# Scores of the last head pair on half the array each: a bucketed attention followed by a channel mix, one core

## The chip, the cores and the metric

The kernel runs on one core of a Trainium2 chip. The metric is the device time of one launch in microseconds (us). The kernel before takes 245.62 us, the median of two runs (245.34 and 245.9). A core has five engines with a queue each: PE (matmul, with its own weight loads), DVE (vector), ACT (activation), POOL (a second, slower vector engine) and SP, which here issues DMAs. Matmuls write to PSUM, 128 partitions of eight banks with 512 float32 columns each; everything else lies in SBUF.

## The reference

Inputs are q, k and v (4 batches, 8 heads, 768 positions, 64 values each), a projection of 64 x 6, and the weights of a channel mix. Each query and key gets a 6-bit bucket from the signs of its projection. Attention is restricted to pairs of equal buckets:

```python
q_bucket = np.sum(q_bits * powers, axis=-1)          # q_bits = (q @ proj) > 0
mask = q_bucket[:, :, :, None] == k_bucket[:, :, None, :]
scores = scale * np.matmul(q, k.transpose(0, 1, 3, 2))
scores = np.where(mask, scores, -1000000000.0)
attn = softmax(scores)                               # written out in the reference
out = np.matmul(attn, v)
```

The heads' outputs are put side by side (x, 4 x 768 x 512), and a channel mix follows:

```python
xk = mu_k * x + (1.0 - mu_k) * x_prev                # x_prev: x one position earlier
xr = mu_r * x + (1.0 - mu_r) * x_prev
k = np.maximum(xk @ w_k, 0.0)
return sigmoid(xr @ w_r) * (k * k @ w_v)
```

## The kernel before, in words

The 32 heads are worked on as 16 pairs (0 to 15), four pairs to a batch. For each pair the kernel does the following.

- **Load and split** (L323, L391, L394). q and k of both heads come in as float32 with 128 partitions. DVE writes a float16 rounding ("hi", 64 columns) and the remainder ("lo", 64 columns) side by side into `nh`. For pairs 4 to 15 one instruction each covers q and k of both heads, 1536 columns.
- **Transpose** (L398). One DMA transposes `nh` to `a`: for each of four blocks (q of head 0, q of head 1, k of head 0, k of head 1) 128 rows by 768 positions, hi in rows 0 to 63 and lo in rows 64 to 127.
- **Bucket bits** (L418, L421, L438). PE multiplies the four blocks with the projection, each on 32 columns of the array, DVE turns the result's signs into values of fixed size, and POOL copies six rows per block over rows 64 to 69 of `a`, over part of lo. One matmul over 128 rows then gives the score plus a bucket term that is large where all six signs agree.
- **Scores** (`add_scores`, L522 to L546). The transposed scores of a pair, 2 heads x 6 key chunks of 128 x 768 queries, are 9216 columns. They are made in nine steps of 1024 columns, named sc15_0 to sc15_8 for pair 15, each into a slot of two PSUM banks. Columns run through head 0 first, then head 1, so a step is cut at every 512 and 768 columns: two or three matmuls (L536). One ACT instruction per step takes the exponential and writes it to `pt` (L540).
- **PV** (`add_pv`, L548 to L613). For each head three groups of twelve matmuls, two key chunks in each (L563): weights are 128 x 128 blocks of `pt`, and 65 columns (v and a column of ones) stream. Head 0 needs steps 0 to 4, head 1 steps 4 to 8. DVE divides by the sum (L576, L577, L581). The result is transposed by a DMA (L597) or, for pair 15 and the first four, on PE (L591).
- **Mix** (`add_mix`, `add_moe`). DVE makes xk and xr (L622 to L636). After a batch's four pairs the channel mix runs: L651 (keys), L671 (gates) and L684 (values) on PE, ACT's relu and tanh (L655, L674), DVE's square and product (L658, L691), and the output DMAs (L694).

The order of the work is written out by hand: every operation gets a number as it is added to a plan, and the list `ORDER` (L17) names all of them in the order in which they are issued, engine by engine first in, first out. `BANKS` (L72) names the PSUM place of each result. The durations that `add` gets play no part in the order. Around pair 15 the order interleaves its nine score steps, one at a time, with those of pairs 13 and 14, PV groups, and the channel mix of batches 1 and 2. Pair 15's steps stand in the order 2, 6, 1, 5, 3, 4, 0, 7, 8. Behind step 7 follow PV's first group of head 1, three groups of head 0, step 8, eight L684, PV's second group of head 1, four L671, and PV's last group.

Of the kernel before, what the change touches and what calls it, by code (L numbers as in the profile page):

```python
# [8 lines left out]
FP32 = mybir.dt.float32  # L9
# [3 lines left out]
AF = mybir.ActivationFunctionType  # L13
ALU = mybir.AluOpType
# [66 lines left out]
]  # L81

# [46 lines left out]
def kernel(  # L129
# [35 lines left out]
    FIRSTS = (0, 1)  # L165
    ROW_SP = ()
    OT_PE = (0, 1, 2, 3, 15)
    QS = 4.0
    ESC = (D ** -0.5) / (QS * QS)
    BITW = 4096.0  # L170
# [13 lines left out]
    nh_t = [buf([P, 4 * NSC, P], FP16, f"nh{i}") for i in range(NNH)]  # L184
    a_t = [buf([P, 4, S], FP16, f"a{i}") for i in range(NAQ)]
    side_nat = {s: [t[:, 2 * i : 2 * i + 2, :] for t in nat_t] for i, s in enumerate("qk")}
    side_nh = {s: [t[:, 2 * NSC * i : 2 * NSC * (i + 1), :] for t in nh_t] for i, s in enumerate("qk")}
    side_a = {s: [t[:, 2 * i : 2 * i + 2, :] for t in a_t] for i, s in enumerate("qk")}
    bx_t = [buf([P, S], FP16, f"bx{i}") for i in range(NBX)]
# [117 lines left out]
    def add_load(n):  # L307
        b, t = divmod(n, NPB)
        s = n % NQ
        for side in "qk":  # L310
            if n == 0:
                for j in range(2):
                    lq = "ACT" if side == "k" and j == 0 else "SP"

                    def f(side=side, j=j, lq=lq):
                        (nc.scalar if lq == "ACT" else nc.sync).dma_start(out=side_nat[side][s][:, j, :],
                                      in_=SRC[side][b, 2 * t + j].rearrange("(p c) d -> p (c d)", c=NSC))
                        if lq == "ACT":
                            nc.scalar.dma_start(out=pj, in_=proj)
                    add(lq, 0.42, f, at=0.75, w=[("nat", side, s, j)] + (["pj"] if lq == "ACT" else []), svc=0.5, name=f"ldq{n}{side}{j}")  # L320
            else:
                def f(side=side):
                    nc.sync.dma_start(out=side_nat[side][s],  # L323
                                      in_=SRC[side][b, 2 * t : 2 * t + 2].rearrange("j (p c) d -> p j (c d)", c=NSC))
                add("SP", 0.5, f, at=0.75, w=[("nat", side, s, j) for j in range(2)], svc=1.05, name=f"ldq{n}{side}")

        def fv():
            nc.sync.dma_start(out=vn_t[n % NV],
                              in_=v[b, 2 * t : 2 * t + 2].rearrange("j (p c) d -> p j (c d)", c=NSC))
        add("SP", 0.5, fv, at=0.75, w=[("vn", n % NV)], svc=1.05, name=f"ldv{n}")  # L330
# [52 lines left out]
    def add_prep(n):  # L383
        s, sh, sa = n % NQ, n % NNH, n % NAQ
        whole = n in MERGED
        for side in ("qk",) if whole else "qk":
            nat, nh, a = (nat_t[s], nh_t[sh], a_t[sa]) if whole else (side_nat[side][s], side_nh[side][sh], side_a[side][sa])
            m = len(side)

            def hi(nat=nat, nh=nh):  # L390
                nc.vector.tensor_scalar(out=nh[:, :, 0:D], in0=nat.rearrange("p j (c d) -> p (j c) d", d=D), scalar1=QS, scalar2=None, op0=ALU.mult)  # L391

            def lo(nat=nat, nh=nh):
                nc.vector.scalar_tensor_tensor(out=nh[:, :, D:P], in0=nat.rearrange("p j (c d) -> p (j c) d", d=D),  # L394
                                               scalar=QS, in1=nh[:, :, 0:D], op0=ALU.mult, op1=ALU.subtract)

            def tr(nh=nh, a=a):
                nc.sync.dma_start_transpose(out=a.rearrange("p j (c q) -> p (j c) q", q=P), in_=nh.rearrange("p c d -> p (c d)"))  # L398
            rn = [("nat", x, s, j) for x in side for j in range(2)]
            nh_h = [("nhh", x, sh, j) for x in side for j in range(2)]  # L400
            nh_l = [("nhl", x, sh, j) for x in side for j in range(2)]
            ax = [("a", x, sa, j) for x in side for j in range(2)] + [("ab", x, sa, j, h) for x in side for j in range(2) for h in range(2)]
            add("DVE", DVE_C(768 * m, 2), hi, r=rn, w=nh_h, port=1, name=f"hi{n}")
            add("DVE", DVE_C(768 * m), lo, r=rn + nh_h, w=nh_l + [("nz", sh)], port=1, name=f"lo{n}")
            add("SP", 1.86 if whole else 1.46, tr, r=nh_h + nh_l, w=ax, svc=2.95 if whole else 1.57, tr=1, name=f"tr{n}")
        add_bits(n, [("q", 0), ("q", 1), ("k", 0), ("k", 1)])

    def add_bits(n, blocks):
# [4 lines left out]
        def f(nm=nm):  # L413
            ps = ps_t[plan.slot[nm]]
            for w_, st in ((p1, True), (p2, False)):
                for lo, hi in ((0, 512), (512, S)):
                    for i, (side, j) in enumerate(blocks):
                        nc.tensor.matmul(ps[32 * i : 32 * i + 32, lo:hi], w_, side_a[side][sa][:, j, lo:hi], start=st, stop=not st)  # L418

        def g(nm=nm):  # L420
            nc.vector.tensor_scalar(  # L421
# [7 lines left out]
        for i, (side, j) in enumerate(blocks):  # L429
            w = [("ab", side, sa, j, h) for h in range(2)]  # L430
            if n in ROW_SP:
                def row(i=i, side=side, j=j):
                    nc.sync.dma_start(out=side_a[side][sa][D : D + NB, j, :], in_=bx_t[sx][32 * i : 32 * i + NB, :])
                add("SP", 0.72, row, r=[("bx", sx)], w=w, svc=0.17, name=f"row{n}{side}{j}")
                continue

            def row(i=i, side=side, j=j):
                nc.gpsimd.tensor_copy(side_a[side][sa][D : D + NB, j, :].bitcast(FP32), bx_t[sx][32 * i : 32 * i + NB, :].bitcast(FP32))  # L438
            add("POOL", 0.55, row, r=[("bx", sx)], w=w, port=1, name=f"row{n}{side}{j}")

    def add_prep_turn(n):
# [74 lines left out]
    def pieces(s):  # L516
# [2 lines left out]
                      | {x for x in range(0, 2 * NSC * S + 1, S) if lo < x < hi})  # L519
        return list(zip(cuts[:-1], cuts[1:]))  # L520

    def add_scores(n):  # L522
        sa, sp = n % NAQ, n % NPT
        for s in range(NSTEP):
            nm = f"sc{n}_{s}"
# [22 lines left out]
    def add_pv(n):  # L548
# [3 lines left out]
        for j in range(2):  # L552
            nm = f"oo{n}_{j}"
            for g in range(3):
                def f(nm=nm, j=j, g=g):
                    oo = sm(nm)
                    if uc and g == 0:
                        nc.tensor.matmul(oo[:, 0:390].rearrange("p (c e) -> p c e", e=65), tiny,
                                         vsu_t[n % NVS][:, j, :].unsqueeze(1).to_broadcast([P, NSC, D + 1]), start=True, stop=False)
                    for jc in (2 * g, 2 * g + 1):  # L560
                        for ic in range(NSC):
                            o = j * NSC * S + jc * S + ic * P
                            nc.tensor.matmul(oo[:, ic * 65 : ic * 65 + 65], pt_t[sp][:, o : o + P], va_t[sa][:, j, jc, 0 : D + 1],  # L563
                                             start=(not uc and ic == 0 and jc == 0), stop=(ic == NSC - 1 and jc == NSC - 1))
                lo = j * NSC * S + 2 * g * S
                steps = range(lo // STEP, (lo + 2 * S - 1) // STEP + 1)
                add("PE", 12 * 0.0315, f, r=[("pt", sp, s) for s in steps] + [("va", sa, j), ("va1", sa)] + (["tiny", ("vs", n % NVS)] if uc else []),
                    w=[(nm,)], take=("sm", nm, 0) if g == 0 else None, name=nm)
            sr = (2 * n + j) % NRC
# [195 lines left out]
```

## Time and profile before

| | |
|---|---|
| median of two runs | 245.62 us (245.34 to 245.9) |
| span of the profiled execution, first to last instruction | 243.0 us |
| time outside the span, median less span | 2.6 us |
| PE busy | 234.2 us, 96% |
| DVE busy | 187.6 us, 77% |
| ACT busy | 182.6 us, 75% |
| POOL busy | 95.9 us, 39% |
| L536, matmuls of the scores, 384 in all, 24 of them pair 15's | 79.2 us with overlaps |
| granted PE clock over the span | 1.000 |

The profile is of one execution, and no time of it other than its span is given. Times in its rows are counted from the first instruction. Lines L... are those of the kernel before. Matmuls are pipelined: the next starts before the last has run out, so durations of PE's rows overlap, and what a matmul costs is read from one start to the next. A value in brackets at a row's end is the idle time of the engine before it and what ended it.

### The profile page before, as it was taken

Reading aid. Unit: us, or ns where it says so; the run is one execution under the profiler, and the core shown is the slowest. Engines: PE = TensorE matmul, PEld = TensorE weight load, DVE = VectorE, ACT = ScalarE, POOL = GpSimd, SP = SyncE. Lnnn points to the kernel's source line nnn. Section 1 sums busy time; section 2 is a strip of 40 time slices with the busy share of each in tenths; the row PEclk is TensorE's granted clock in tenths of the full one; section 3 lists DMA queues with packets and bytes.
Section 4 is the critical chain, followed back from the end, with each engine's and each line's share of the span. In section 5 each row is a group of like instructions: output and inputs, shape, how many; then the busy total and the mean of one; then the engine's idle time right before and its main releaser. Section 6 shows DMA issues by size and latency. Waiting matters only on the chain.

```text
span 243.0 us, 6250 instructions
## 1 busy us (share of the span) xinstructions
PE 234.2 (96%) x2522; PEld 147.3 (61%) x2522; DVE 187.6 (77%) x388; ACT 182.6 (75%) x242; POOL 95.9 (39%) x150
## 2 busy tenths in 40 slices
PE   8998999999999899999999999999999999999994
PEld 6975676765567446465556665465566765455443
DVE  3489899999899989699999989936745476966142
ACT  3689999999989689698877998777679871165230
POOL 5465797885919673428036230093500000000000
PEclk9999999999999999999999999999999999999999
DMA  6989999999999999999989683464310403041033
GB/s 229 370 243 197 219 259 230 356 204 348 245 217 233 367 281 208 259 272 264 222 195 233 155 162 85 146 114 126 120 46 0 35 3 119 0 173 47 0 131 132
DMA packets 72526, 44.01 MB, mean 181 GB/s; under 512 B 54832, under 2 KB 67504, under 8 KB 72496
## 3 DMA queue, kind: packets, MB, share of 16 engines
q1 hardware_dynamic: 72272, 43.40, 70.7%
q8 instruction: 20, 0.33, 0.6%
q10 hardware_dynamic: 224, 0.20, 0.2%
q14 instruction: 10, 0.08, 0.1%
HBM read 24.12 MB, written 6.29 MB: 125 GB/s over the span
## 4 chain that ended last, share of the span: by engine, by line
PE 55%; DVE 6%; DMA 3%; issue 1%; DVEq 0%
PE ps_all L684 15%; PE ps_all L651 13%; PE ps_all L536 11%; PE ps_all L671 8%; PE ps_all L563 6%; DMA a<-nh 3%; PE ps_all L418 2%; DVE xk L636 1%; DVE tm L633 1%; DVE nh L391 1%; DVE nh L394 1%; DVE df L622 0%; DVE os L691 0%; DVE va L373 0%; DVE bx L421 0%
## 5 line engine op out<-in xcount | busy, mean ns | idle before, releaser
L540 ACT ACTIVATE pt<-ps_all 128x1024 bf16<-128x1024 f32 x144 | 139.1, 1040 | 19.8 <-PE ps_all L536 18.7
L536 PE MATMUL ps_all<-a 128*128 128x256 f16 (+1 forms) x384 | 79.2, 325 | 2.0 <-ACT pt L540 1.1
L438 POOL COPY a<-bx 6x384 f32<-6x384 f32 x56 | 38.9, 696 | 54.5 <-DVE bx L421 42.3
L563 PEld LDWEIGHTS <-pt 128*128 128x128 bf16 x1152 | 43.7, 97 | 11.6 <-issue 2.1
L651 PE MATMUL ps_all<-xk,wk 128*128 128x384 bf16 x256 | 49.6, 326 | 0.3 <-DVE xk L636 0.3
L536 PEld LDWEIGHTS <-a 128*128 128x128 f16 x384 | 33.7, 98 | 24.9 <-issue 3.5
L684 PE MATMUL ps_all<-wv,k 128*128 128x512 bf16 (+2 forms) x208 | 46.7, 363 | 0.0
L563 PE MATMUL ps_all<-va,pt 128*128 128x65 bf16 x1152 | 46.2, 193 | 0.4 <-DVE va L373 0.4
L658 DVE TENSOR_TENSOR k<-kr 128x384 bf16<-128x384 bf16 x64 | 25.8, 424 | 14.1 <-ACT kr L655 13.8
L655 ACT ACTIVATE kr<-ps_all 128x384 bf16<-128x384 f32 x64 | 29.6, 497 | 7.7 <-PE ps_all L651 6.7
L651 PEld LDWEIGHTS <-wk 128*128 128x128 bf16 x256 | 24.0, 98 | 15.5 <-issue 0.3
L674 ACT ACTIVATE rs<-ps_all 128x512 f32<-128x512 f32 x24 | 14.3, 603 | 23.0 <-DVE os L691 11.7
L684 PEld LDWEIGHTS <-k 128*128 128x128 bf16 x208 | 19.6, 98 | 19.1
L691 DVE SCALAR_TENSOR_TENSOR os<-rs,ps_all 128x512 f32<-128x512 f32 (+2 forms) x26 | 16.7, 643 | 14.9 <-PE ps_all L684 10.8
L394 DVE SCALAR_TENSOR_TENSOR nh<-nat,nh 128x1536 f16<-128x1536 f32 (+1 forms) x16 | 25.7, 1607 | 0.2
L671 PE MATMUL ps_all<-wr,xr 128*128 128x512 bf16 x96 | 24.5, 379 | 0.0
L349 POOL TENSOR_TENSOR vt<-vn 128x384 f32<-128x384 f32 x12 | 14.4, 1200 | 10.8 <-DMA vn<-in_v_dram 7.1
L581 DVE TENSOR_TENSOR ob<-ps_all,rc 128x384 bf16<-128x384 f32 x32 | 17.5, 552 | 0.7
L391 DVE TENSOR_SCALAR nh<-nat 128x1536 f16<-128x1536 f32 (+1 forms) x16 | 15.8, 989 | 1.5 <-DMA nat<-in_k_dram 0.9
L671 PEld LDWEIGHTS <-xr 128*128 128x128 bf16 x96 | 8.7, 97 | 9.5 <-issue 0.6
L421 DVE TENSOR_SCALAR bx<-ps_all 128x768 uint16<-128x768 uint16 x14 | 13.3, 952 | 1.2 <-PE ps_all L418 0.8
L373 DVE SCALAR_TENSOR_TENSOR va<-ps_all,vn 128x384 bf16<-128x384 f32 x24 | 12.8, 549 | 1.4 <-ACT pt L540 0.9
(77 smaller groups left out, 190.6 us busy)
## 6 DMA issues: line engine op xcount, KB each, us to landing
vn<-in_v_dram SPq DMA_DIRECT2D x16, 384.0 KB, 5.1
out_dram<-os SPq DMA_DIRECT2D x23, 256.0 KB, 2.5
nat<-in_q_dram SPq DMA_DIRECT2D x15, 384.0 KB, 4.6
nat<-in_k_dram SPq DMA_DIRECT2D x15, 384.0 KB, 5.3
wst<-in_moe_w_k_dram SPq DMA_DIRECT2D x2, 512.0 KB, 7.2
wst<-in_moe_w_r_dram SPq DMA_DIRECT2D x2, 512.0 KB, 6.2
wst<-in_moe_w_v_dram SPq DMA_DIRECT2D x2, 512.0 KB, 5.9
k<-in_moe_w_k_dram SPq DMA_DIRECT2D x1, 512.0 KB, 7.8
```

Source lines behind the costliest of these rows:

```text
L391: nc.vector.tensor_scalar(out=nh[:, :, 0:D], in0=nat.rearrange("p j (c d) -> p (j c) d", d=D), scalar1=QS, scalar2=None, op0=ALU.mult)
L394: nc.vector.scalar_tensor_tensor(out=nh[:, :, D:P], in0=nat.rearrange("p j (c d) -> p (j c) d", d=D), scalar=QS, in1=nh[:, :, 0:D], op0=AL ...
L438: nc.gpsimd.tensor_copy(side_a[side][sa][D : D + NB, j, :].bitcast(FP32), bx_t[sx][32 * i : 32 * i + NB, :].bitcast(FP32))
L536: nc.tensor.matmul(ps[:, lo - s * STEP : hi - s * STEP], side_a["k"][sa][:, j, jc * P : (jc + 1) * P], side_a["q"][sa][:, j, q0 : q0 + hi ...
L540: nc.scalar.activation(out=pt_t[sp][:, s * STEP : (s + 1) * STEP], in_=ps_t[plan.slot[nm]], func=AF.Exp, bias=EBIAS, scale=ESC)
L563: nc.tensor.matmul(oo[:, ic * 65 : ic * 65 + 65], pt_t[sp][:, o : o + P], va_t[sa][:, j, jc, 0 : D + 1], start=(not uc and ic == 0 and jc ...
L581: nc.vector.tensor_tensor(out=ob_t[so][:, :, j * D : (j + 1) * D], in0=oo[:, :, 0:D], in1=rc_t[sr][:, 1, :].unsqueeze(2).to_broadcast([P, ...
L651: nc.tensor.matmul(ps[:, 0:HALF], wk_sb[:, d, fc * P : (fc + 1) * P], xk_t[mx[d]][:, h * HALF : (h + 1) * HALF], start=(d == 0), stop=(d = ...
L655: nc.scalar.activation(out=kr_t[sk], in_=sm(nm)[:, 0:HALF], func=AF.Relu, scale=0.5 ** 0.5)
L658: nc.vector.tensor_tensor(out=k2_t[s2][:, h * HALF : (h + 1) * HALF], in0=kr_t[sk], in1=kr_t[sk], op=ALU.mult)
L671: nc.tensor.matmul(sm(nr), xr_t[mx[d]][:, c * P : (c + 1) * P], wr_sb[:, d, :], start=(d == 0), stop=(d == NDC - 1))
L684: nc.tensor.matmul(sm(nv)[:, x0:x1], k2_t[(b * NFC + fc) % NK2][:, c * P : (c + 1) * P], wv_sb[:, fc, x0:x1], start=(fc == 0), stop=(fc == ...
```

## The change

For pair 15 alone (`TILED = (15,)`), the two heads are laid on different halves of the array's rows.

- The four blocks are stored in the order q of head 0, k of head 0, q of head 1, k of head 1 (`til_nat`, `til_a`), and head 1 has its hi in rows 64 to 127 and its lo in rows 0 to 63. DVE's hi and lo are two instructions of 768 columns each instead of one of 1536. The six bucket rows of head 1 go to rows 0 to 5 and those of head 0 to rows 64 to 69.
- A score step holds 512 columns of head 0 in one bank of the slot and 512 of head 1 in the other. Steps 0, 1 of every three are one key chunk by the first 512 queries, step 2 the last 256 queries of both chunks. A step is a matmul of 64 rows per head and key chunk, and then one of six rows per head and key chunk that adds the bucket term: 4 or 8 matmuls instead of 2 or 3, each with its weight load, 48 instead of 24 for the pair.
- The lo part is not used in the scores of this pair. Before, lo rows 70 to 127 stood in the sum with lo of the other side.
- PV reads `pt` by the new places. Each group g of either head needs steps 3g, 3g+1 and 3g+2.
- `ORDER` keeps the places of the steps and their exps, which now run from 0 to 8 in turn. In PE's queue, head 0's third PV group stands behind step 8, where it stood ahead of it.

```diff
-    ... 1220, 1216, 1221, 1217, 1218, 998, ...
+    ... 1220, 1216, 1217, 1218, 1221, 998, ...
```

In these numbers 1220 and 1221 are head 0's second and third PV group, 1216 is the exp of step 7, 1217 and 1218 are step 8 and its exp, and 998 is the first four of the eight L684.

```diff
+    til_nat = {s: [t.rearrange("p (j i) x -> p i j x", i=2)[:, i] for t in nat_t] for i, s in enumerate("qk")}
+    til_a = {s: [t.rearrange("p (j i) x -> p i j x", i=2)[:, i] for t in a_t] for i, s in enumerate("qk")}
...
+            def split(nat, nh):
+                x = nat.rearrange("p j (c d) -> p (j c) d", d=D)
+                if n not in TILED:
+                    return [(x, nh[:, :, 0:D], nh[:, :, D:P])]
+                h = 2 * NSC
+                return [(x[:, 0:h], nh[:, 0:h, 0:D], nh[:, 0:h, D:P]), (x[:, h:], nh[:, h:, D:P], nh[:, h:, 0:D])]
+
             def hi(nat=nat, nh=nh):
-                nc.vector.tensor_scalar(out=nh[:, :, 0:D], in0=nat.rearrange("p j (c d) -> p (j c) d", d=D), scalar1=QS, scalar2=None, op0=ALU.mult)
+                for x, h, _ in split(nat, nh):
+                    nc.vector.tensor_scalar(out=h, in0=x, scalar1=QS, scalar2=None, op0=ALU.mult)
...
             def row(i=i, side=side, j=j):
+                d0 = 0 if n in TILED and j == 1 else D
...
+    def add_scores_tiled(n):
+        sa, sp = n % NAQ, n % NPT
+        qa, ka = til_a["q"][sa], til_a["k"][sa]
+        for s in range(NSTEP):
+            nm = f"sc{n}_{s}"
+            i, r = divmod(s, 3)
+            parts = [(2 * i + r, 0, 512, 0)] if r < 2 else [(2 * i + e, 512, 256, 256 * e) for e in range(2)]
+
+            def f(nm=nm, parts=parts):
+                ps = ps_t[plan.slot[nm]]
+                for x, (jc, q0, w, o) in enumerate(parts):
+                    for j in range(2):
+                        rows = slice(j * D, (j + 1) * D)
+                        nc.tensor.matmul(ps[:, j * 512 + o : j * 512 + o + w], ka[rows, j, jc * P : (jc + 1) * P], qa[rows, j, q0 : q0 + w],
+                                         start=(x == 0), stop=False)
+                for x, (jc, q0, w, o) in enumerate(parts):
+                    for j in range(2):
+                        rows = slice(0, NB) if j else slice(D, D + NB)
+                        nc.tensor.matmul(ps[:, j * 512 + o : j * 512 + o + w], ka[rows, j, jc * P : (jc + 1) * P], qa[rows, j, q0 : q0 + w],
+                                         start=False, stop=(x == len(parts) - 1))
...
+            add("PE", STEP / 2400.0 + 0.2, f, r=[("ab", x, sa, j, h) for x in "qk" for j in range(2) for h in range(2)] + [("a", x, sa, j) for x in "qk" for j in range(2)],
+                w=[(nm,)], take=("sc", nm, 0), name=nm)
+            add("ACT", ACT_C(STEP), g, r=[(nm,)], w=[("pt", sp, s)], give=[nm], name=f"exp{n}_{s}")
+
+    def place(n, j, jc, ic):
+        if n not in TILED:
+            return j * NSC * S + jc * S + ic * P
+        i, e = divmod(jc, 2)
+        return (3 * i + e) * STEP + j * 512 + ic * P if ic < 4 else (3 * i + 2) * STEP + j * 512 + e * 256 + (ic - 4) * P
...
-                            o = j * NSC * S + jc * S + ic * P
+                            o = place(n, j, jc, ic)
...
-                steps = range(lo // STEP, (lo + 2 * S - 1) // STEP + 1)
+                steps = range(3 * g, 3 * g + 3) if n in TILED else range(lo // STEP, (lo + 2 * S - 1) // STEP + 1)
```

More of the change, by code (lines that the diff above doesn't have):

```diff
@@ L167 @@
     OT_PE = (0, 1, 2, 3, 15)
+    TILED = (15,)
     QS = 4.0
@@ L322, in f @@
                 def f(side=side):
-                    nc.sync.dma_start(out=side_nat[side][s],
+                    nc.sync.dma_start(out=(til_nat if n in TILED else side_nat)[side][s],
                                       in_=SRC[side][b, 2 * t : 2 * t + 2].rearrange("j (p c) d -> p j (c d)", c=NSC))
@@ L388, in add_prep @@
             m = len(side)
+            def split(nat, nh):
[4 more added lines that the diff above has]
+                return [(x[:, 0:h], nh[:, 0:h, 0:D], nh[:, 0:h, D:P]), (x[:, h:], nh[:, h:, D:P], nh[:, h:, 0:D])]
             def hi(nat=nat, nh=nh):
-                nc.vector.tensor_scalar(out=nh[:, :, 0:D], in0=nat.rearrange("p j (c d) -> p (j c) d", d=D), scalar1=QS, scalar2=None, op0=ALU.mult)
+                for x, h, _ in split(nat, nh):
+                    nc.vector.tensor_scalar(out=h, in0=x, scalar1=QS, scalar2=None, op0=ALU.mult)
             def lo(nat=nat, nh=nh):
-                nc.vector.scalar_tensor_tensor(out=nh[:, :, D:P], in0=nat.rearrange("p j (c d) -> p (j c) d", d=D),
-                                               scalar=QS, in1=nh[:, :, 0:D], op0=ALU.mult, op1=ALU.subtract)
+                for x, h, l in split(nat, nh):
+                    nc.vector.scalar_tensor_tensor(out=l, in0=x, scalar=QS, in1=h, op0=ALU.mult, op1=ALU.subtract)
             def tr(nh=nh, a=a):
@@ L417, in f @@
                     for i, (side, j) in enumerate(blocks):
-                        nc.tensor.matmul(ps[32 * i : 32 * i + 32, lo:hi], w_, side_a[side][sa][:, j, lo:hi], start=st, stop=not st)
+                        nc.tensor.matmul(ps[32 * i : 32 * i + 32, lo:hi], w_, (til_a if n in TILED else side_a)[side][sa][:, j, lo:hi], start=st, stop=not st)
         def g(nm=nm):
@@ L437, in row @@
             def row(i=i, side=side, j=j):
-                nc.gpsimd.tensor_copy(side_a[side][sa][D : D + NB, j, :].bitcast(FP32), bx_t[sx][32 * i : 32 * i + NB, :].bitcast(FP32))
+                d0 = 0 if n in TILED and j == 1 else D
+                nc.gpsimd.tensor_copy((til_a if n in TILED else side_a)[side][sa][d0 : d0 + NB, j, :].bitcast(FP32), bx_t[sx][32 * i : 32 * i + NB, :].bitcast(FP32))
             add("POOL", 0.55, row, r=[("bx", sx)], w=w, port=1, name=f"row{n}{side}{j}")
@@ L520, in pieces, with g @@
         return list(zip(cuts[:-1], cuts[1:]))
+    def add_scores_tiled(n):
[17 more added lines that the diff above has]
+                                         start=False, stop=(x == len(parts) - 1))
+            def g(nm=nm, s=s):
+                nc.scalar.activation(out=pt_t[sp][:, s * STEP : (s + 1) * STEP], in_=ps_t[plan.slot[nm]],
+                                     func=AF.Exp, bias=EBIAS, scale=ESC)
+            add("PE", STEP / 2400.0 + 0.2, f, r=[("ab", x, sa, j, h) for x in "qk" for j in range(2) for h in range(2)] + [("a", x, sa, j) for x in "qk" for j in range(2)],
[6 more added lines that the diff above has]
+        return (3 * i + e) * STEP + j * 512 + ic * P if ic < 4 else (3 * i + 2) * STEP + j * 512 + e * 256 + (ic - 4) * P
     def add_scores(n):
+        if n in TILED:
+            add_scores_tiled(n)
+            return
         sa, sp = n % NAQ, n % NPT
```

12 rows, old and new, of tables (BANKS, ORDER) are left out of this document.

## The prediction

> **What bounds the kernel now.** I read the page first, then the stages, then the time around the last pair. The page gives each engine's busy time and, in 40 slices, its share and the granted clock.
>
> ```profile
> span 243.0 us, 6250 instructions
> PE 234.2 (96%) x2522; PEld 147.3 (61%) x2522; DVE 187.6 (77%) x388; ACT 182.6 (75%) x242; POOL 95.9 (39%) x150
> PE   8998999999999899999999999999999999999994
> PEclk9999999999999999999999999999999999999999
> ```
>
> PE is busy for 96% of the span at full clock. An average can hide stages, so the second view cuts the stretch in which pairs 13 to 15 are scored (columns: stretch, length, busy time of PE, its weight loads, DVE, ACT, POOL, then clock and DMA).
>
> ```profile
> 140.00:160.00 20.00, 20.00 (x198) 11.59 (x197) 17.87 (x42) 17.32 (x24) 4.00 (x5) 1.00 0.52 119
> 160.00:180.00 20.00, 20.00 (x216) 12.20 (x214) 10.99 (x26) 14.94 (x20) 8.74 (x16) 1.00 0.45 111
> 180.00:195.00 15.00, 15.00 (x169) 9.74 (x167) 7.82 (x27) 13.04 (x21) 0.00 (x0) 1.00 0.21 31
> 195.00:199.50 4.50, 4.50 (x76) 3.18 (x74) 3.27 (x11) 3.42 (x4) 0.00 (x0) 1.00 0.02 4
> 199.50:201.25 1.75, 1.75 (x10) 0.80 (x9) 1.09 (x4) 1.02 (x1) 0.00 (x0) 1.00 0.00 0
> 201.25:212.00 10.75, 10.75 (x77) 5.50 (x76) 9.32 (x22) 0.75 (x2) 0.00 (x0) 1.00 0.22 67
> 212.00:240.00 28.00, 27.66 (x160) 14.80 (x158) 13.12 (x31) 11.88 (x25) 0.00 (x0) 1.00 0.25 95
> ```
>
> From 140 to 212 us PE has not one idle row, and 0.34 us of idle after that. So two things hold for this change: no wait of PE is left in its neighbourhood that it could remove, and whatever it adds to PE's queue, streaming or waiting, moves the end by as much, since PE's later work has nothing idle to absorb it.
>
> The third view is PE's and ACT's rows in order of time around pair 15's last two score steps (start, length, what, count; an ACT L540 is one exp of 1024 columns).
>
> ```profile
> 196.32 1.02 PE L671 MATMUL ps_all<-wr,xr 128*128 128x512 bf16 x4
> 197.18 0.59 PE L536 MATMUL ps_all<-a 128*128 128x512 f16 x2
> 197.38 0.60 ACT L674 ACTIVATE rs<-ps_all 128x512 f32<-128x512 f32 x1 [0.20 <-PE ps_all L671]
> 197.61 1.62 PE L563 MATMUL ps_all<-va,pt 128*128 128x65 bf16 x48
> 197.87 1.02 ACT L540 ACTIVATE pt<-ps_all 128x1024 bf16<-128x1024 f32 x1
> 199.07 0.60 PE L536 MATMUL ps_all<-a 128*128 128x256 f16 x3
> 199.50 1.89 PE L684 MATMUL ps_all<-wv,k 128*128 128x512 bf16 x8
> 199.70 1.02 ACT L540 ACTIVATE pt<-ps_all 128x1024 bf16<-128x1024 f32 x1 [0.81 <-PE ps_all L536]
> 201.23 0.53 PE L563 MATMUL ps_all<-va,pt 128*128 128x65 bf16 x12
> ```
>
> Start to start, a score step of 1024 columns holds PE 0.43 us (197.18 to 197.61), eight matmuls of 512 columns 1.73 (199.50 to 201.23, 0.216 each), and 48 PV matmuls 1.46, so a group of 12 takes 0.365. The 1.62 us of the PV row is longer only because the row includes the last matmul's run-out.
>
> **The change, part by part.**
>
> *Streaming.* A score step was two matmuls of 512 columns (or 256, 512, 256). It becomes two of 64 rows, one per head, then two of 6 rows on 32-row tiles. If both heads of a pair stream side by side, that is 512 columns twice, 2 x 0.216 = 0.43 us: as before. Nothing is saved even at best, since the bucket rows that used to ride in the same 128 rows now need a pass of their own. No row of this trace has a tile of 64 or 32 rows of the array; the nearest are the bucket bits at L418, four tiles of 32 columns of the array.
>
> ```profile
> 153.60 1.03 PE L684 MATMUL ps_all<-wv,k 128*128 128x512 bf16 x4
> 154.56 0.83 PE L418 MATMUL ps_all<-a,p 128*32 128x512 f16 x16
> 155.33 0.60 PE L671 MATMUL ps_all<-wr,xr 128*128 128x512 bf16 x2
> ```
>
> Sixteen matmuls, eight of 512 and eight of 256 columns, take 0.77 us; one after another they would take 8 x 0.324 = 2.6. So tiles do stream side by side, four at a time in 0.65 (2 x 0.324), and I take the same for two row tiles. The Trainium skill, "TensorE: Matmul & The Clock Gate", Measured speedup, gives 3.07 times for four row tiles of 32 rows and 512 columns. By that figure a pass costs 1.3 times one matmul, and 18 passes would add, as an estimate, 1.2 us to the sum; no run here shows it.
>
> *Changes of tile form.* The same rows show what it costs to go in and out. The four L684 before the bits take 0.96 instead of 0.86 us, and the bits 0.77 instead of 0.65: 0.21 for two changes, 0.105 each. After every step PE returns to 128-row work, so a step has three changes (128 to 64, 64 to 32, back): 0.315 us. Ends for one change: nothing, if weights load behind the running matmul as they do within one form; and 0.26, from these rows:
>
> ```profile
> L536 PE MATMUL ps_all<-a 128*128 128x512 f16 x192 | 62.1, 379 | 1.6 <-DVE ob L581 0.8 <-ACT pt L540 0.7
> L536 PE MATMUL ps_all<-a 128*128 128x256 f16 x192 | 36.2, 272 | 0.4 <-ACT pt L540 0.4
> L536 PEld LDWEIGHTS <-a 128*128 128x128 f16 x384 | 33.7, 98 | 24.9 <-issue 3.5 <-POOL wv L299 1.1 <-POOL vt L352 0.5
> ```
>
> A matmul lasts 379 ns though its successor starts after 216: 0.163 of run-out, plus 0.098 for a weight load. I take 0.105, the only measured change. Seven steps (0 to 6) lie between other PE work: 7 x 0.315 = 2.2 us.
>
> *The order of the last PV groups.* Steps now hold both heads, so PV's third group of either head needs the last exp. In PE's queue head 0's third group, which stood ahead of the last score step, now stands straight behind it. PE takes its matmuls in order; its first four read exps 6 and 7 and go on, the fifth waits for exp 8, and behind it stand the eight L684, the remaining PV and all of the channel mix. Before, the L684 and nothing else covered that exp. Two more rows, of an earlier stage, give PE's answer to an exp's end.
>
> ```profile
> 17.71 1.95 ACT L540 ACTIVATE pt<-ps_all 128x1024 bf16<-128x1024 f32 x2
> 19.71 0.38 PE L536 MATMUL ps_all<-a 128*128 128x256 f16 x2 [0.38 <-ACT pt L540]
> ```
>
> The exp ends at 19.66, the waiting matmul starts at 19.71: 0.05. ACT in turn starts 0.03 after the matmul's row ends (199.67 to 199.70). Counted from the start of step 7:
>
> - step 7: change 0.105, pass 0.216, change 0.105, last pass starts at 0.43, leaves PE at 0.75; its matmul ends at 0.82, exp 7 runs 0.85 to 1.87;
> - three PV groups (one fewer than before): 0.75 to 1.84;
> - step 8 uses the slot that exp 7 reads, free at 1.92; with the change in, it starts at 1.95. Passes of 0.216, change 0.105, the last matmul of 256 columns starts at 2.38 and ends 0.27 later, 2.65; exp 8 runs 2.68 to 3.70;
> - the fifth PV matmul starts at 3.75, eight of them take 0.25: L684 starts at 4.00.
>
> Before, L684 started 2.32 after step 7 (197.18 to 199.50). So +1.68 us: about 0.6 changes of form, about 1.05 a new wait in PE's queue.
>
> *DVE, POOL, DMA.* Pair 15's hi and lo are each cut in two.
>
> ```profile
> L394 DVE SCALAR_TENSOR_TENSOR nh<-nat,nh 128x1536 f16<-128x1536 f32 x12 | 21.8, 1816 | 0.1
> L391 DVE TENSOR_SCALAR nh<-nat 128x1536 f16<-128x1536 f32 x12 | 12.3, 1027 | 0.9 <-DMA nat<-in_k_dram 0.9
> L394 DVE SCALAR_TENSOR_TENSOR nh<-nat,nh 128x768 f16<-128x768 f32 x4 | 3.9, 980 | 0.1
> L391 DVE TENSOR_SCALAR nh<-nat 128x768 f16<-128x768 f32 x4 | 3.5, 875 | 0.6 <-PE ps_all L504 0.6
> 157.66 1.75 DVE L394 SCALAR_TENSOR_TENSOR nh<-nat,nh 128x1536 f16<-128x1536 f32 x1
> 163.25 1.02 DVE L658 TENSOR_TENSOR k<-kr 128x384 bf16<-128x384 bf16 x2 [3.84 <-ACT kr L655]
> 172.75 1.32 POOL L438 COPY a<-bx 6x384 f32<-6x384 f32 x2
> 182.22 0.60 PE L536 MATMUL ps_all<-a 128*128 128x256 f16 x3
> ```
>
> By the means of the halves (taken early, among DMA) that is at most 2 x 0.875 - 1.03 + 2 x 0.98 - 1.82 = 0.86 us, at least nothing. DVE then idles 3.84 us, which hides it; without that cover it would delay pair 15's transposing DMA and its bits by up to 0.86. The first step now needs all four bucket copies instead of two: the last ends at 174.07 on POOL, 8.1 us before the step at 182.22, so nothing. Loads and copies keep their sizes and their places. Head 0's divide and its share of the tail now follow the new wait, but PE's own later work is shifted as far, and DVE's slack against it stays.
>
> **Sum.** 2.2 + 1.68 = 3.9 us on a profiled span of 243.0; the runs' median is 245.62, 2.6 of it outside the span, which the change does not touch. 245.6 + 3.9 = **249.5 us**, 1.6% longer.
>
> **The rivals.**
>
> *Row tiles take turns.* Each pass is then two matmuls in a row, a step 0.43 longer: 7 x 0.75 = 5.2. At the tail L684 starts at 4.86 by the same count, +2.54. Together +7.8: 253.4. For it: no row shows two row tiles at once, and both write all 128 output columns. Against it: L418's overlap.
>
> *A change of form runs PE empty*, 0.26 each: 7 x 0.78 = 5.5, L684 at 4.76, +2.44; together +7.9: 253.5. L418's 0.105 speaks against it. The Trainium skill, "TensorEngine Tiling (Array Packing)", Key Properties, says that changing the tiling mode drains the TensorE; a full drain would be this rival, and by the 0.105 that rows show the trace agrees only in part.
>
> *Changes cost nothing here*: only the new wait. Exp 7 cannot start before ACT's tanh is out of the way (0.69), L684 starts at 3.7, +1.4: 247.0. For it: weight loads hide within one form. Against: the measured 0.105.
>
> *Not slower: all four tiles of a step in flight together.* If the 6-row tiles streamed beside the 64-row ones without a change, a step would hold PE 0.22: 7 x 0.22 = 1.5 saved, L684 at 3.5, +1.2: -0.3, so 245.3. It turns from about 0.25 us per step down, where the seven steps pay for the wait. Against it: head 0's six rows lie at row 64, inside head 1's tile, and so busy.
>
> **How the numbers follow.** Forecast 0.62 (its own range 248.4 to 250.8), cheap changes 0.15, turns 0.10, running empty 0.09, four together 0.04. Low 246.9 takes in cheap changes; high 251.8 takes in passes at 1.3 and half of what lies towards 253.5; what is left out is some 2 in 10. Two per cent, about what a measurement of this kernel can tell from no change, lies at 250.5 above and 240.7 below. Slower by over 2%: both costly rivals and a little of the forecast's upper end, 0.24. Faster by over 2%: 0.01. Within: 0.75.
>
> **What would show it.** In the changed kernel's time order: pair 15's steps (two lines in place of L536) 0.75 us start to start, matmuls of one pass starting a few ns apart; before and after them 0.1 us in which PE starts nothing. After the last step four PV matmuls, then an idle row of PE of about 1 us ended by ACT's exp, the only one between 140 and 212 us; ACT's last exp ending about 4 us later than now. Two L394 and L391 of 768 columns with DVE still idle behind them. I am wrong if the passes' matmuls start 0.2 us apart, if a change takes over 0.2 or under 0.05, or if PE starts other work while the fifth PV matmul waits.

## The result, and the profile after

The changed kernel takes 249.32 us (median of two runs, 249.29 to 249.36) against 245.62: 1.0144 times before, 95% interval 1.0107 to 1.0182. Measured again, six runs beside 17 of before, it took 249.97 against 246.26, a ratio of 1.0185 (1.0139 to 1.0231). So it is slower, by 1% to 2.3%; 249.5 was forecast.

The profiled execution's span grew by 4.62 us, from 243.0 to 247.6, more than the median's 3.70. Part of that does not come from the score steps, as two rows of each kernel show: PE's bucket bits of pair 15, which come before all of pair 15's scores, and DVE's last product, behind which only output DMAs run. First before, then after (time order; start, length, what).

```profile
169.08 0.83 PE L418 MATMUL ps_all<-a,p 128*32 128x512 f16 x16
239.70 0.29 DVE L691 SCALAR_TENSOR_TENSOR os<-rs,ps_all 128x128 f32<-128x128 f32 x1 [0.16 <-PE ps_all L684]
```

```profile
169.78 0.83 PE L429 MATMUL ps_all<-a,p 128*32 128x512 f16 x16
244.32 0.29 DVE L740 SCALAR_TENSOR_TENSOR os<-rs,ps_all 128x128 f32<-128x128 f32 x1 [0.16 <-PE ps_all L733]
```

From the start of the bits to the start of the last product it is 70.62 us before and 74.54 after: 3.92 us more. The other 0.70 us came before the bits; the third set of bits already starts at 37.01 instead of 36.13 us, where both programs still do the same. Runs differ in that early part; the stretch behind the bits repeats: in the second profile of the changed kernel it is 74.54 again (170.17 to 244.71). So I compare kernels by this stretch and give the medians beside it; it is read from one profile of each kernel, and from two of the changed one. What keeps the median's growth at 3.70 is the time outside the span: 2.6 us by the median before, but 1.76 (249.36 less 247.6) in the changed kernel's profiled run. It is not fixed for one kernel either: in 23 runs of before on one chip it was 1.7 to 2.7 us.

The next view is the changed kernel's PE in order of time around two steps of pair 15, and its weight loads in the same stretch. L547 is the pass of 64 rows, L552 that of six rows, L612 PV, L733 the value matmuls.

```profile
182.12 0.59 PE L585 MATMUL ps_all<-a 128*128 128x512 f16 x2
182.55 0.53 PE L612 MATMUL ps_all<-va,pt 128*128 128x65 bf16 x12
183.01 0.39 PE L547 MATMUL ps_all<-a 64*128 64x512 f16 x2
183.33 0.39 PE L552 MATMUL ps_all<-a 6*128 6x512 f16 x2
183.65 1.04 PE L733 MATMUL ps_all<-wv,k 128*128 128x512 bf16 x4
184.62 0.39 PE L547 MATMUL ps_all<-a 64*128 64x512 f16 x2
184.95 0.39 PE L552 MATMUL ps_all<-a 6*128 6x512 f16 x2
185.27 0.82 PE L700 MATMUL ps_all<-xk,wk 128*128 128x384 bf16 x4
```

```profile
183.01 0.10 PEld L547 LDWEIGHTS <-a 64*128 64x128 f16 x2
183.33 0.10 PEld L552 LDWEIGHTS <-a 6*128 6x128 f16 x2 [0.23 <-issue]
183.65 0.55 PEld L733 LDWEIGHTS <-k 128*128 128x128 bf16 x4 [0.23 <-issue]
```

A pass of two matmuls lasts 0.39 us, hardly longer than one alone: the heads stream side by side. But from one pass to the next it is 0.32 us (183.01, 183.33, 183.65), not the 0.216 that 512 columns take, and each form's first weight load is recorded only as its pass starts. Within one form the loads run ahead: the four of L733 are done at 184.20, its four matmuls stream until 184.52. Going in costs the same 0.1: 12 PV matmuls that take 0.365 elsewhere take 0.46 here, four L733 0.97 instead of 0.86. A step holds PE 0.75 us instead of 0.43.

The last view is the end of the scores, PE first, then ACT.

```profile
199.24 1.02 PE L720 MATMUL ps_all<-wr,xr 128*128 128x512 bf16 x4
200.20 0.39 PE L547 MATMUL ps_all<-a 64*128 64x512 f16 x2
200.52 0.39 PE L552 MATMUL ps_all<-a 6*128 6x512 f16 x2
200.84 1.27 PE L612 MATMUL ps_all<-va,pt 128*128 128x65 bf16 x36
202.04 0.39 PE L547 MATMUL ps_all<-a 64*128 64x256 f16 x4
202.36 0.39 PE L552 MATMUL ps_all<-a 6*128 6x256 f16 x4
202.68 0.30 PE L612 MATMUL ps_all<-va,pt 128*128 128x65 bf16 x4
203.87 0.42 PE L612 MATMUL ps_all<-va,pt 128*128 128x65 bf16 x8 [0.89 <-ACT pt L556]
...
205.85 0.53 PE L612 MATMUL ps_all<-va,pt 128*128 128x65 bf16 x12
```

```profile
200.95 1.02 ACT L556 ACTIVATE pt<-ps_all 128x1024 bf16<-128x1024 f32 x1
202.79 1.02 ACT L556 ACTIVATE pt<-ps_all 128x1024 bf16<-128x1024 f32 x1 [0.82 <-PE ps_all L552]
```

Four PV matmuls go, and the fifth stands until the exp of step 8 ends at 203.81. Before, this place in PE's rows had no idle time at all. One of the eight L733 records is missing in this trace, so their first start is counted back from the next PV: 205.85 - 8 x 0.216 = 204.12.

### The profile page after: what moved, and what is told of

Same layout as the page of the kernel before. It is cut to its first block, busy times and chain, and to the rows that moved or that the text cites. A ratio compares the mean times of both kernels' runs of the same rounds, so it can differ in the third digit from the quotient of the medians.

```text
span 247.6 us, 6283 instructions
## 1 busy us (share of the span) xinstructions
PE 236.5 (96%) x2529; PEld 146.4 (59%) x2546; DVE 188.4 (76%) x390; ACT 183.1 (74%) x242; POOL 94.7 (38%) x150
## 4 chain that ended last, share of the span: by engine, by line
PE 68%; ACT 12%; DVE 8%; DMA 6%; issue 3%; POOL 2%; SPq 0%; DVEq 0%; POOLq 0%; ACTq 0%
PE ps_all L733 15%; PE ps_all L700 15%; PE ps_all L585 13%; ACT pt L589 11%; PE ps_all L612 8%; PE ps_all L720 8%; PE ps_all L429 3%; DMA nat<-in_k_dram 2%; DMA a<-nh 2%; PE ps_all L493 2%; DMA nat<-in_q_dram 2%; PE ps_all L552 1%; PE ps_all L547 1%; DVE bx L432 1%; DVE xk L685 1%
## 5 line engine op out<-in xcount | busy, mean ns | idle before, releaser
L589 ACT ACTIVATE pt<-ps_all 128x1024 bf16<-128x1024 f32 x135 | 130.4, 1040 | 18.4 <-PE ps_all L585 17.1
L585 PE MATMUL ps_all<-a 128*128 128x256 f16 (+1 forms) x360 | 74.1, 325 | 2.7 <-DVE ob L630 1.5
L450 POOL COPY a<-bx 6x384 f32<-6x384 f32 x56 | 40.1, 719 | 56.7 <-DVE bx L432 44.1
L612 PEld LDWEIGHTS <-pt 128*128 128x128 bf16 x1152 | 43.5, 97 | 13.3 <-issue 3.3
L612 PE MATMUL ps_all<-va,pt 128*128 128x65 bf16 x1152 | 46.6, 193 | 1.4 <-ACT pt L556 0.9
L733 PE MATMUL ps_all<-wv,k 128*128 128x512 bf16 (+2 forms) x198 | 45.5, 362 | 0.5
L585 PEld LDWEIGHTS <-a 128*128 128x128 f16 x360 | 31.5, 98 | 24.0 <-issue 4.0
L733 PEld LDWEIGHTS <-k 128*128 128x128 bf16 x208 | 19.3, 98 | 19.1 <-issue 0.4
L406 DVE SCALAR_TENSOR_TENSOR nh<-nat,nh 128x1536 f16<-128x1536 f32 (+1 forms) x17 | 27.1, 1600 | 0.2
L720 PE MATMUL ps_all<-wr,xr 128*128 128x512 bf16 x89 | 23.6, 379 | 0.4
L352 POOL TENSOR_TENSOR vt<-vn 128x384 f32<-128x384 f32 x12 | 13.3, 1108 | 10.1 <-DMA vn<-in_v_dram 9.5
L402 DVE TENSOR_SCALAR nh<-nat 128x1536 f16<-128x1536 f32 (+1 forms) x17 | 15.0, 888 | 0.8 <-PE ps_all L516 0.6
L720 PEld LDWEIGHTS <-xr 128*128 128x128 bf16 x96 | 8.7, 97 | 9.5 <-issue 0.6
```

What stands on the lines that cost most here:

```text
L406: nc.vector.scalar_tensor_tensor(out=l, in0=x, scalar=QS, in1=h, op0=ALU.mult, op1=ALU.subtract)
L450: nc.gpsimd.tensor_copy((til_a if n in TILED else side_a)[side][sa][d0 : d0 + NB, j, :].bitcast(FP32), bx_t[sx][32 * i : 32 * i + NB, :].b ...
L585: nc.tensor.matmul(ps[:, lo - s * STEP : hi - s * STEP], side_a["k"][sa][:, j, jc * P : (jc + 1) * P], side_a["q"][sa][:, j, q0 : q0 + hi ...
L589: nc.scalar.activation(out=pt_t[sp][:, s * STEP : (s + 1) * STEP], in_=ps_t[plan.slot[nm]], func=AF.Exp, bias=EBIAS, scale=ESC)
L720: nc.tensor.matmul(sm(nr), xr_t[mx[d]][:, c * P : (c + 1) * P], wr_sb[:, d, :], start=(d == 0), stop=(d == NDC - 1))
L733: nc.tensor.matmul(sm(nv)[:, x0:x1], k2_t[(b * NFC + fc) % NK2][:, c * P : (c + 1) * P], wv_sb[:, fc, x0:x1], start=(fc == 0), stop=(fc == ...
```

## The experiments

For every kernel the stretch is from the start of pair 15's bits to the start of the last DVE product, read from the two rows as above; "over before" is against 70.62 us.

| kernel | stretch, us | over before | ratio of times (95%) |
|---|---|---|---|
| changed | 74.54, 74.54 | +3.92 | 1.0144 (1.0107 to 1.0182), 1.0185 (1.0139 to 1.0231) |
| PV group behind the value matmuls | 73.47 | +2.85 | 1.0115 (1.0088 to 1.0141) |
| no tiles | 72.02 | +1.40 | 1.0058 (1.0035 to 1.0081) |
| no tiles and PV group moved | 70.85 | +0.23 | 1.0029 (1.0004 to 1.0053) |
| five changes of form a step | 76.46 | +5.84 | 1.0261 (1.0232 to 1.0289) |
| second pass in the same form | 73.59 | +2.97 | 1.0128 (1.0089 to 1.0167) |
| no second pass | 71.79 | +1.17 | 1.0055 (1.0029 to 1.0080) |

My theory was the prediction's: 2.84 us of changes of form (27 at 0.105) and some 1.05 us of a new wait in PE's queue. The rivals were costs in the layout or in the tail, and a price that is of the visit or of row tiles as such.

**The wait alone.** Head 0's third PV group (1221) goes behind the eight value matmuls, and the last multiplication of pair 14's divide (1185, DVE) ahead of pair 15's divide (1222), so that the latter does not hold it up.

```diff
-    1220, 1216, 1217, 1218, 1221, 998, 986, 999, 1225, 1086, 1222, 1185, 1223, 1000,
+    1220, 1216, 1217, 1218, 998, 986, 999, 1221, 1225, 1086, 1185, 1222, 1223, 1000,
```

> The changed kernel, with head 0's third PV group of pair 15 moved in PE's queue behind the eight value matmuls that follow step 8 (and DVE's product of pair 14 moved ahead of pair 15's divide). My account (nine steps with three changes of tile form at 0.105 us each, 2.84 us, and 1.05 us of a wait in PE's queue): the idle row of PE before the fifth PV matmul is gone, and the time falls from 249.3 by 1.05 to 248.3 us. Rival, the wait is only handed on: DVE's divide and mix of pair 15 now come later and the channel mix of the last batch waits for them; then it stays at 248.9 to 249.3 and an idle row of PE stands before the first key matmul of the last batch.

The median was 248.8 us against 246.29 of before on that chip. PE in order of time in this kernel:

```profile
202.40 0.39 PE L552 MATMUL ps_all<-a 6*128 6x256 f16 x4
202.72 1.90 PE L733 MATMUL ps_all<-wv,k 128*128 128x512 bf16 x8
204.46 0.89 PE L612 MATMUL ps_all<-va,pt 128*128 128x65 bf16 x24
205.19 1.02 PE L720 MATMUL ps_all<-wr,xr 128*128 128x512 bf16 x4
```

The value matmuls start right behind step 8 and cover the exp; the 24 PV matmuls that follow do not wait. The stretch is 1.07 us shorter than the changed kernel's, and no idle row of PE appears later, so the wait was not handed on to the channel mix. The median stands 2.51 above its own before, where 2.7 had been expected. By the medians alone a fall of 1.05 us would not be told from noise; by the stretch it is.

**The tiles alone.** Layout, slots, halves and order stay; each score matmul goes over all 128 rows.

```diff
-                        rows = slice(j * D, (j + 1) * D)
-                        nc.tensor.matmul(ps[...], ka[rows, j, jc * P : (jc + 1) * P], qa[rows, j, q0 : q0 + w],
-                                         start=(x == 0), stop=False)
-                for x, (jc, q0, w, o) in enumerate(parts):
-                    for j in range(2):
-                        rows = slice(0, NB) if j else slice(D, D + NB)
-                        nc.tensor.matmul(ps[...], ka[rows, j, jc * P : (jc + 1) * P], qa[rows, j, q0 : q0 + w],
-                                         start=False, stop=(x == len(parts) - 1))
+                        nc.tensor.matmul(ps[...], ka[:, j, jc * P : (jc + 1) * P], qa[:, j, q0 : q0 + w],
+                                         start=True, stop=True)
```

> The changed kernel with everything as it is (layout of the blocks, halves of hi and lo, slots with 512 columns of each head, order), but each score matmul goes over all 128 rows, hi, lo and bucket rows in one pass: 24 matmuls in place of 48. My account: the 27 changes of form go, 2.84 us, the wait grows by about 0.35 us since step 8 is sooner ready than ACT, so 246.8 us (1.2 to 1.4 above before). Rival, the cost lies in the layout and the order and not in the tiles: 248.5 or more.

The median was 247.36 us, 1.07 above its own before; the stretch is 1.40 us above. PE's rows:

```profile
197.91 0.59 PE L546 MATMUL ps_all<-a 128*128 128x512 f16 x2
198.34 1.26 PE L606 MATMUL ps_all<-va,pt 128*128 128x65 bf16 x36
199.68 0.60 PE L546 MATMUL ps_all<-a 128*128 128x256 f16 x4
200.11 0.28 PE L606 MATMUL ps_all<-va,pt 128*128 128x65 bf16 x4
201.39 0.42 PE L606 MATMUL ps_all<-va,pt 128*128 128x65 bf16 x8 [0.99 <-ACT pt L550]
```

A step is 0.43 us again, and the wait is there and a little longer. With it comes a second, small one: 36 PV matmuls from 198.34 would be done at 199.43, but step 8 starts at 199.68, 0.05 after exp 7, which reads its slot, ends at 199.63 in ACT's rows. The tiles had hidden that: there the 36 PV matmuls and the change of form end at 202.04, when the slot is free (exp 7 ends at 201.97).

**Both edits.** 

> Both edits together: matmuls over all 128 rows, and head 0's third PV group behind the eight value matmuls. My account: nothing of the 3.7 us is left, 245.6 us, within 0.4 of before. Rival, a third cost that I have put at nothing (the halves of hi and lo on DVE, four bucket copies before the first step, both heads ending together): what remains above 246.0 is that.

The median was 246.88 against 246.29, 0.59 above and so outside the 0.4 that was expected, with a ratio whose interval just leaves out 1; the stretch is 0.23 us above before. The rows, PE and then ACT, name what is left in the stretch.

```profile
198.28 0.59 PE L546 MATMUL ps_all<-a 128*128 128x512 f16 x2
198.71 1.26 PE L606 MATMUL ps_all<-va,pt 128*128 128x65 bf16 x36
200.04 0.60 PE L546 MATMUL ps_all<-a 128*128 128x256 f16 x4
200.48 1.89 PE L727 MATMUL ps_all<-wv,k 128*128 128x512 bf16 x8
```

```profile
198.48 0.60 ACT L717 ACTIVATE rs<-ps_all 128x512 f32<-128x512 f32 x1 [0.20 <-PE ps_all L714]
198.97 1.02 ACT L550 ACTIVATE pt<-ps_all 128x1024 bf16<-128x1024 f32 x1
```

Between steps 7 and 8 stand 36 PV matmuls (1.09 us) where 48 (1.46) stood before. They end at 199.80, and step 8 waits for its slot until 200.04, 0.05 after exp 7 ends: 0.24. Exp 7 in turn follows the tanh (L717) that ACT takes first. So the four bucket copies and heads that end together cost nothing in this stretch; all that is left of the 3.92 us is this wait for a slot.

The halves on DVE come before the bits, so the stretch cannot show their cost. PE's rows ahead of the bits can, first in before, then in this kernel.

```profile
168.63 0.53 PE L563 MATMUL ps_all<-va,pt 128*128 128x65 bf16 x12
169.08 0.83 PE L418 MATMUL ps_all<-a,p 128*32 128x512 f16 x16
```

```profile
169.73 0.53 PE L606 MATMUL ps_all<-va,pt 128*128 128x65 bf16 x12
170.19 0.83 PE L429 MATMUL ps_all<-a,p 128*32 128x512 f16 x16
```

The bits start 0.45 to 0.46 us after the PV matmuls ahead of them in both, and neither kernel has an idle row of PE from 140 us to its bits: the bits did not wait for the split. The rest of the median's 0.59 lies outside the stretch and was not traced to a cause.

**More changes of form.** Each step is cut into two halves of 256 columns a head, each with both its passes.

```diff
+                if len(parts) == 1:
+                    jc, q0, w, o = parts[0]
+                    cut = [(jc, q0, 256, o), (jc, q0 + 256, 256, o + 256)]
+                else:
+                    cut = parts
+                for x, (jc, q0, w, o) in enumerate(cut):
+                    for hi in (True, False):
+                        for j in range(2):
+                            rows = slice(j * D, (j + 1) * D) if hi else slice(0, NB) if j else slice(D, D + NB)
...
```

> The changed kernel with each step cut in two halves of 256 columns per head, each with its pass of 64 rows and its pass of 6 rows, so that a step has five changes of tile form in place of three; the columns that stream are the same. My account, a price per change of 0.105 us: 18 more changes, 1.9 us, 251.2 us, and rows of 0.21 us from one pass's start to the next. Rival, the price is of the visit (in and out) and not of each change: 249.3 to 249.7 us.

The median was 252.51 us against 246.29, 6.2 above, where 5.6 had been expected. The stretch is 1.92 us longer than the changed kernel's, 18 changes at 0.107. Both passes have one line in this kernel, so its rows merge them:

```profile
183.96 0.93 PE L553 MATMUL ps_all<-a 64*128 64x256 f16 x8
184.82 1.04 PE L734 MATMUL ps_all<-wv,k 128*128 128x512 bf16 x4
```

Four passes of 256 columns take 0.86 us, 0.215 each, where 256 columns stream in 0.108. So the price is of each change, and is the same with 256 columns between two changes as with 512.

**Two passes in one form.** The second pass reads the same 64 rows again, so this kernel leaves the bucket term out.

```diff
-                        rows = slice(0, NB) if j else slice(D, D + NB)
+                        rows = slice(j * D, (j + 1) * D)
```

> The changed kernel, with the second pass of each step over the same 64 rows as the first (hi again) in place of the six bucket rows: the scores are doubled and the bucket term is left out, and the same columns stream in the same number of matmuls, but a step has two changes of tile form in place of three. If the price is that weights for another form are not loaded ahead, the second pass starts 0.22 us after the first and not 0.32, a step takes 0.64 us, and PE's time from pair 15's bits to its last matmul is 2.9 us above before, 1.0 below the changed kernel: about 248.5 us where before takes 245.6. Rival, row tiles never load weights ahead, whatever the form: the passes stay 0.32 apart and the time that of the changed kernel, 249.3.

The median was 248.77 us against 246.26. PE, then its weight loads:

```profile
183.98 0.39 PE L547 MATMUL ps_all<-a 64*128 64x512 f16 x2
184.21 0.38 PE L552 MATMUL ps_all<-a 64*128 64x512 f16 x2
184.52 0.66 PE L700 MATMUL ps_all<-xk,wk 128*128 128x384 bf16 x3
```

```profile
183.98 0.10 PEld L547 LDWEIGHTS <-a 64*128 64x128 f16 x2 [0.42 <-issue]
183.99 0.10 PEld L552 LDWEIGHTS <-a 64*128 64x128 f16 x2
184.51 0.44 PEld L700 LDWEIGHTS <-wk 128*128 128x128 bf16 x4 [0.42 <-issue]
```

The second pass starts 0.23 us after the first, and its weights are loaded at 183.99, while the first pass streams over the same rows. So row tiles do load ahead within one form; across a change, no load stands ahead of its pass in the rows shown. The stretch is 0.95 us shorter than the changed kernel's: nine changes fewer, 0.105 each. The bucket rows themselves were not put on the 64-row form: there a head's scores and its bucket term would come from different halves of the array's rows and be added into one bank, and whether that works was not tried.

**No second pass.** The changed kernel with the second pass, and so the bucket term, left out.

```diff
-                                         start=(x == 0), stop=False)
-                for x, (jc, q0, w, o) in enumerate(parts):
-                    ...
+                                         start=(x == 0), stop=(x == len(parts) - 1))
```

> The changed kernel without the second pass: no bucket term, so 24 matmuls of 64 rows, two changes of form per step, half of the streaming of before. My account: a step takes 0.216 + 2 x 0.105 = 0.43 us, as much as two matmuls over 128 rows, so that packing two heads gains nothing even where no bucket pass follows; only the wait of PE's queue is left, 1.2 us above before, 246.8. Rival, the changes of form are cheaper where no second pass of 32 rows follows: a step of 0.3 us or less, and 245.7 or less.

The median was 247.51 us against 246.26, the stretch 1.17 us above before.

```profile
183.08 1.04 PE L728 MATMUL ps_all<-wv,k 128*128 128x512 bf16 x4
184.05 0.39 PE L547 MATMUL ps_all<-a 64*128 64x512 f16 x2
184.37 0.82 PE L695 MATMUL ps_all<-xk,wk 128*128 128x384 bf16 x4
```

Four L728 from 183.08 stream until 183.94; the next 128-row work starts at 184.37: 0.43 us for a step that streams 512 columns, just what two matmuls over 128 rows take. Packing saves 0.216 us of streaming a step and two changes give it back.

**The changed kernel again**, beside the last two:

> The changed kernel once more, beside the two above on one chip: 3.7 to 3.9 us above before, and PE's time from pair 15's bits to its last matmul 3.9 us above before.

It gave 249.97 us, 3.71 above its before, and the same stretch as the first profile.

No version beats before: the one nearest to it has neither the tiles nor the wait.

## Why the prediction was right

- *Streaming, the same at best.* Right. Two row tiles start 3 to 4 ns apart in the trace's records, and a pass without a change before the next takes 0.23 us (183.98 to 184.21), not the 0.43 of two matmuls in a row. The rival in which row tiles take turns is out, and so is that in which all four tiles fly together. The Trainium skill, "TensorE: Matmul & The Clock Gate", Measured speedup vs the span model, gives 3.07 times for four row tiles, from which I estimated a pass at 0.28 us (1.3 x 0.216); for two tiles of 64 rows the trace does not bear that out.
- *Changes of form, 0.105 each, 2.84 in all.* Right, though taken from column tiles: 2.85 us is what is left without the wait, and 18 more changes cost 1.92, nine fewer save 0.95. The rival of a PE that runs empty (0.26) is out by its size. The Trainium skill, "TensorEngine Tiling (Array Packing)", Key Properties, says that a change of tiling mode drains the TensorE; what these runs show of it is 0.1 us in which no new matmul starts. What PE does in that time, no run shows.
- *The order of the last PV groups, 1.05.* Right: 1.07 went when the group was moved. The steps of that count also hold: the fifth PV matmul 3.75 us after step 7's start was expected, 3.77 is in the rows (200.10, the end of streaming of four L720 from 199.24, to 203.87), and the value matmuls at 4.00 against 4.02.
- *DVE, POOL, DMA, nothing.* Right as far as the rows go. The two halves of lo took 2.12 us instead of 1.75 and DVE then idled 3.46 instead of 3.84; the last bucket copy ended at 174.77, 8.2 us before the first step. With tiles and wait gone nothing of them is left in the stretch, and the bits did not wait for the split.
- *The size.* 3.9 us was the sum, 3.92 the stretch, 3.70 the medians. The stretch is the test of the sum. That the median came within 0.2 of 249.5 is partly luck: the prediction took the part ahead of the bits and the 2.6 us outside the span as fixed, and by the numbers above the first grew by 0.70 and the second shrank by 0.8, which nearly cancels.

One step was loose: I counted the slot that step 8 takes over from step 7 as free in time (1.92 against 1.95), which holds only with the tiles. Without them it is late by 0.24 us, which the rival "changes cost nothing here" did hold in its count, and the expectation for both edits did not.

## What to carry to other kernels

Where PE has no idle row for tens of microseconds, count what a change adds to its queue, streams, changes of form and waits alike; here that count was the time (3.9 against 3.92), and nothing later gave it back. Packing two half-height matmuls onto the array halved their streaming, but each change of tile form cost about 0.1 us on PE, so short visits between full-height work gained nothing: at 512 columns a visit in and out just broke even, and a third change was all loss. And when a new layout makes two results ripen together, look for what used to be done while the last of them was on its way: here one place in an order written out by hand cost as much as ten changes of form.

## What the runs showed of the hardware that I had not expected

The price of a change hardly depended on the forms: from 128 rows to 64, from 64 to six, from six to 128, and back and forth between 64 and six all cost 0.10 to 0.11 us, the same as the column tiles of the bucket bits, and about the 0.10 us that one weight load lasts; whether it is that load was not shown. And the kernel's execution time varies by up to 2.4 us between runs of before on one chip (245.23 to 247.65), over twice the cost of the new wait, while the stretch behind pair 15's bits is 74.54 in both profiles of the changed kernel: between those two, what varies lies ahead of it (bits at 169.78 and 170.17). In the one place that I followed, at 37 us, PE waited 0.23 us for a transposing DMA that it did not wait for before; why the early part varies was not tried.
